# Sketched attention and a tanh-shrink layer pair: values loaded by head onto 96 partitions, q of the first batch split, and four small early reads

## The chip, the core and the metric

The kernel runs on one core of one Trainium2 chip. The core has a matrix engine (TensorE, PE in the profile), a vector engine (VectorE, DVE), a scalar engine (ScalarE, ACT), GpSimd (POOL), and SyncE (SP), which here only issues transfers; sixteen DMA engines move data between device memory and on-chip memory. The metric is the time of one execution in device microseconds, less is better.

## The reference

For four batches, four heads, 1088 tokens and head size 32, a linear attention with a sketched feature map comes first; its output, laid out as 4352 tokens of width 128, goes through two layers with h - tanh(h) between them.

```
def phi(x):                              # S1, S2: 8 x 32
    a = einsum('rd,bhsd->bhsr', S1, x)
    b = einsum('rd,bhsd->bhsr', S2, x)
    return einsum('bhsi,bhsj->bhsij', a, b).reshape(..., 64)
kv  = einsum('bhsf,bhsd->bhfd', phi(k), v)
z   = sum(phi(k), axis=2)
num = einsum('bhsf,bhfd->bhsd', phi(q), kv)
den = einsum('bhsf,bhf->bhs', phi(q), z)[..., None] + 1e-06
x   = (num / den).transpose(0, 2, 1, 3).reshape(4352, 128)
h   = x @ w_in                           # 128 x 2048
out = (h - tanh(h)) @ w_out              # 2048 x 128
```

All inputs and the output are float32.

## The kernel before

The kernel is a program of 753 operations, each put on one engine. The function `op` derives what each operation must wait for from the tiles that it reads and writes, `sync` turns that into semaphore waits, and `run` issues each engine's operations strictly in the order of a list (`ORDER`), which was written out beforehand by the planner in `schedule` from costs and due times. An engine that waits holds everything behind it in its list. Negative numbers in TensorE's list are idle matmuls on zeros.

**Loads.** All large loads are issued by SyncE in one queue: `load_k`, `load_q`, `load_v` for each batch, and four parts each of w_in and w_out (`load_w_in`, `load_w_out`). `load` keeps a list of the bytes asked for, `flow`, and makes a load wait until those more than 1,900,000 bytes ahead of it have landed (`AHEAD`). k and q come as 128 partitions (4 heads x 32 blocks j of 34 tokens), each one run of 4352 bytes; k of batch 0 comes in two parts. v comes in four transfers, one for each quarter c of the 34 tokens of a block: 32 partitions (the blocks j), and in each of them four heads with a run of nine tokens, 1152 bytes (seven tokens, 896 bytes, for the last quarter). On chip v lies as `vx`, partition 32 c + j, then head, token in the quarter, and 32 values. ScalarE's queue issues only the two small loads of S1 and S2 (`load_s`), ahead of the load of its tanh table.

**Attention.** k is transposed in 32 x 32 blocks by VectorE (L567, L710 for batch 0), projected by TensorE (L522), turned back (`kab`, L530), and multiplied out by GpSimd (`wk`, L558; for batch 0 partly VectorE); L585 sums `wk` against `vx`. q is transposed by VectorE (`q_transpose`, L608), projected (L624), turned back (`qf`, L631), and gives the denominators (`dt` L637, `den` L640, `rec` L643), the scaled factors (`an` L651), their products by GpSimd (`qp` L660), and the transposes of these (`qpT` L665). TensorE forms the numerators (L680), and ScalarE copies them to `xT` as bf16 (L690). The first 256 tokens of batch 0 have a short way of their own (`first_keys`, `first_factors`, `first_sums`, `first_numerators`; x at L799), so that the layers can start early; for them q of batch 0 is transposed in two parts (256 columns, then the rest), from one load. The copy to `sw` at L726 is a step of that way.

**Layers.** The tokens are cut into groups (128, 128, 256, seven of 512, 256). For each, 16 tiles of the first layer (L887) go to tanh on ScalarE (L892), 136 tiles of 128 x 512 in all, and the second layer (L906, L913 for the last group) sums w_out against tanh in one bank; the linear part h is taken care of by the product of the two weight matrices (`whi`, `wlo`; L932, L928). VectorE transposes each group's result out of the bank (L947, L940) and SyncE stores it (L954; the last group at L942). The next group's sums need that bank. w_in is cast by ScalarE (L819), w_out by GpSimd (L823).

Of the kernel before, what the change touches and what calls it, by code (L numbers as in the profile page):

```python
# [10 lines left out]
B, H, S, D = 4, 4, 1088, 32  # L11
# [5 lines left out]
OFF = (0, 9, 18, 27)  # L17
NT = 9
# [2 lines left out]

ORDER = {
    "tensor": (
# [17 lines left out]
    ),  # L41
    "scalar": (
# [9 lines left out]
    ),  # L52
    "vector": (
# [4 lines left out]
    ),  # L58
    "gpsimd": (
        21, 3, 22, 9, 7, 10, 8, 4, 23, 75, 82, 84, 59, 60, 134, 61, 62, 132, 150, 149, 151, 277, 302, 300, 280, 281,  # L60
        283, 285, 301, 431, 454, 456, 434, 435, 437, 439, 455, 579, 582, 583, 585, 587,
    ),
    "sync": (
# [4 lines left out]
    ),  # L68
}

# [256 lines left out]
def bass_polysketch_attn__then__act_tanh_shrink_kernel(nc, q, k, v, S1, S2, moe_w_in, moe_w_out, out):  # L327
    P = Program(nc)

    def sb(name, shape, dtype=F32):  # L330
        return nc.alloc_sbuf_tensor(name, shape, dtype).ap()
# [11 lines left out]
    identb = sb("identb", [128, 128], BF16)  # L343
    wz = sb("wz", [128, 512], BF16)
    spare = sb("spare", [128, 1], BF16)
    m4 = sb("m4", [128, 4])
    m16 = sb("m16", [128, 2, 4])
    e16 = sb("e16", [16, 8, 16])
# [7 lines left out]
    qraw = [sb(f"qraw{i}", [128, S]) for i in range(2)]  # L356
    kT = [sb(f"kT{i}", [128, 4 * NT * 32]) for i in range(2)]
    qT = [sb(f"qT{i}", [128, S]) for i in range(2)]
    vx = [sb(f"vx{i}", [128, H, NT, D]) for i in range(2)]
# [60 lines left out]
    def load_s():  # L420
        for i, src in enumerate((S2, S1)):
            load("scalar", ("s_raw",), "s", 0, lambda e, i=i, src=src: e.dma_start(
                out=s_raw[8 * i:8 * i + 8, :, :], in_=src[:, None, :].to_broadcast([R, H, D])), 4096, True, name="load s")

    def load_k(b, due):
        cuts = ((0, 512), (512, S)) if b == 0 else ((0, S),)
        for x, (lo, hi) in enumerate(cuts):
            load("sync", [("kraw", b % 2, y) for y in ((x,) if b == 0 else (0, 1))], f"k{b}{x}", due, lambda e, lo=lo, hi=hi: e.dma_start(  # L428
                out=kraw[b % 2][:, lo:hi], in_=k[b].rearrange("h (j c) d -> (h j) (c d)", j=32)[:, lo:hi]),
                512 * (hi - lo), rate=400 if b == 0 else 300, name=f"load k{b}")  # L430

    def load_v(b, due):
        src = v[b].rearrange("h (j c) d -> j h c d", j=32)
        for c in range(4):
            n = NT if c < 3 else 7
            load("sync", ("vx", b % 2), f"v{b}{c}", due + c, lambda e, c=c, n=n: e.dma_start(
                out=vx[b % 2][32 * c:32 * c + 32, :, 0:n, :].rearrange("j h t d -> j h (t d)"),
                in_=src[:, :, OFF[c]:OFF[c] + n, :].rearrange("j h t d -> j h (t d)")),
                128 * 128 * n, True, 226, name=f"load v{b}")

    def load_q(b, due):
        i = b % 2
        load("sync", ("qraw", i), f"q{b}", due, lambda e: e.dma_start(
            out=qraw[i][:, :], in_=q[b].rearrange("h (j c) d -> (h j) (c d)", j=32)), 512 * S, name=f"load q{b}")

    def load_w_in(x, due):
        load("sync", ("w_in_f", x), f"wi{x}", due, lambda e: e.dma_start(
            out=w_in_f[:, 512 * x:512 * x + 512], in_=moe_w_in[:, 512 * x:512 * x + 512]), 262144, rate=390, name="load w_in")
# [157 lines left out]
    def q_transpose(b, part, lo, hi):  # L606
        i = b % 2
        P.op("vector", dve(hi - lo), lambda e: e.transpose(out=qT[i][:, lo:hi], in_=qraw[i][:, lo:hi]),  # L608
             r=[("qraw", i)], w=[("qT", i, y) for y in (range(2) if part is None else (part,))], name="qT")

    def layout(nblk):
        nb = (nblk + 3) // 4
# [347 lines left out]
    constants()  # L960
    load_s()
    load_k(0, 100)
    load_q(0, 150)
    load_v(0, 200)
    load_w_in(0, 400)
    load_w_in(1, 450)
    load_w_in(2, 500)
    load_w_in(3, 550)
    load_w_out(0, 650)
    load_w_out(1, 700)  # L970
    load_k(1, 750)
# [14 lines left out]
    for kind, x in steps:  # L986
        x, upto = int(x), 0
# [22 lines left out]
        while g < len(groups) and sum(groups[g]) <= upto:  # L1010
            first_layer(g, *groups[g])
            if g < 2:
                turn_weights(g)
            elif g == 2:
                for y in range(3):
                    second_layer(y, *groups[y])
            else:
                second_layer(g, *groups[g])
            g += 1
    P.emit(lambda e: e.matmul(ps[:, 6, 0:128], wz[:, 0:128], wz[:, 0:128], start=True, stop=True))  # L1020


# [26 lines left out]
```

## Time and profile before

| what | value |
|---|---|
| time, median of 3 runs | 110.84 us (109.92 to 111.91) |
| time of the profiled execution | 111.44 us |
| its span | 109.7 us |
| granted TensorE clock | 0.998 |
| busy: PE, DVE, ACT, POOL | 101.0, 46.5, 84.4, 41.8 us |
| read from device memory, written | 8.79 MB, 2.23 MB |
| tanh on ScalarE (L892) | 136 tiles, 70.3 us |

Busy times are those of one execution; TensorE's are modelled, so a busy TensorE isn't one at its peak. In the stretches that follow, the columns are the stretch, its length, the busy time of PE, PEld (weight loads), DVE, ACT and POOL with the number of instructions, the granted clock, the share of time in which the sixteen DMA engines are busy, on average over them, and GB/s. In a timeline a row has the start, the busy time, the engine, the line, the operation, output and input, and in brackets the idle time ahead of it with what ended it. In the chain a row has the start, the duration and what it was. In the DMA issues the last number is the time from issue to landing.

### The profile page before, as it was taken

Reading aid. Unit: us, or ns where it says so; the run is one execution under the profiler, and the core shown is the slowest. Engines: PE = TensorE matmul, PEld = TensorE weight load, DVE = VectorE, ACT = ScalarE, POOL = GpSimd, SP = SyncE. Lnnn points to the kernel's source line nnn. Section 1 sums busy time; section 2 is a strip of 40 time slices with the busy share of each in tenths; the row PEclk is TensorE's granted clock in tenths of the full one; section 3 lists DMA queues with packets and bytes.
Section 4 is the critical chain, followed back from the end, with each engine's and each line's share of the span. In section 5 each row is a group of like instructions: output and inputs, shape, how many; then the busy total and the mean of one; then the engine's idle time right before and its main releaser. Section 6 shows DMA issues by size and latency. Waiting matters only on the chain.

```text
span 109.7 us, 3290 instructions
## 1 busy us (share of the span) xinstructions
PE 101.0 (92%) x1406; PEld 57.4 (52%) x1406; DVE 46.5 (42%) x88; ACT 84.4 (77%) x184; POOL 41.8 (38%) x46
## 2 busy tenths in 40 slices
PE   5999998898988989999999999999999999999940
PEld 4956677574646734443546543454444444345730
DVE  2737999736859384075017402527600200200210
ACT  3132479765964769798998979999979999999920
POOL 5204435799117998004999500269300000000000
PEclk9999999999999999999999999999999999999999
DMA  2999999996766821023000500410023041032061
GB/s 68 311 234 233 298 324 284 210 318 127 235 219 195 216 47 21 6 37 59 6 0 6 92 7 0 75 26 0 0 46 49 7 75 21 0 57 42 6 96 48
DMA packets 22195, 11.24 MB, mean 102 GB/s; under 512 B 17828, under 2 KB 20004, under 8 KB 22180
## 3 DMA queue, kind: packets, MB, share of 16 engines
q1 hardware_dynamic: 22100, 11.02, 40.9%
q8 instruction: 11, 0.18, 0.8%
q14 instruction: 4, 0.03, 0.1%
q10 hardware_dynamic: 80, 0.01, 0.1%
HBM read 8.79 MB, written 2.23 MB: 100 GB/s over the span
## 4 chain that ended last, share of the span: by engine, by line
PE 46%; DMA 32%; ACT 14%; DVE 2%; SPq 1%; issue 1%; DVEq 0%
PE ps L887 17%; PE ps L906 16%; DMA qraw<-in_q_dram 16%; ACT tt L892 13%; DMA w_out_f<-in_moe_w_out_dram 7%; DMA kraw<-in_k_dram 6%; PE ps L680 4%; DMA w_in_f<-in_moe_w_in_dram 4%; PE ps L932 2%; PE ps L585 2%; PE ps L913 1%; PE ps L624 1%; DVE qT L608 1%; ACT xT L690 1%; SPq L428 1%; PE ps L538 1%
## 5 line engine op out<-in xcount | busy, mean ns | idle before, releaser
L892 ACT ACTIVATE tt<-ps 128x512 bf16<-128x512 f32 x136 | 70.3, 659 | 4.8 <-PE ps L887 4.4
L887 PE MATMUL ps<-xT,w_in 128*128 128x512 bf16 (+2 forms) x176 | 48.1, 335 | 1.3 <-ACT w_inT L849 0.5
L906 PE MATMUL ps<-tt,w_out 128*128 128x512 bf16 (+2 forms) x160 | 41.3, 337 | 0.0
L887 PEld LDWEIGHTS ps<-xT,w_in 128*128 128x128 bf16 x176 | 17.5, 114 | 21.5 <-ACT tt L892 10.6
L947 DVE STREAM_TRANSPOSE osb<-ps 128x512 f32<-128x512 f32 (+2 forms) x10 | 5.9, 587 | 32.5 <-PE ps L906 32.5
L906 PEld LDWEIGHTS ps<-tt,w_out 128*128 128x128 bf16 x160 | 14.6, 99 | 9.1 <-ACT tt L892 0.7
L558 POOL TENSOR_TENSOR wk<-kab 128x768 f32<-128x768 f32 x10 | 15.1, 1508 | 8.9 <-DVE kab L530 8.3
L660 POOL TENSOR_TENSOR qp<-an,qf 128x768 f32<-128x768 f32 (+1 forms) x11 | 16.2, 1470 | 2.1 <-DVE an L651 1.3
L665 DVE STREAM_TRANSPOSE qpT<-qp 128x768 f32<-128x768 f32 (+1 forms) x12 | 11.1, 927 | 10.8 <-POOL qp L660 10.7
L637 POOL TENSOR_TENSOR dt<-qf 128x288 f32<-128x288 f32 x3 | 2.4, 796 | 16.8 <-DVE qf L631 16.8
L1020 PE MATMUL ps<-wz 128*128 128x128 bf16 x81 | 8.2, 256 | 0.0
L1020 PEld LDWEIGHTS ps<-wz 128*128 128x128 bf16 x81 | 6.4, 117 | 2.9 <-issue 2.6
L690 ACT CAST xT<-ps 128x256 bf16<-128x256 f32 (+3 forms) x16 | 5.3, 391 | 2.9 <-PE ps L680 2.9
L608 DVE STREAM_TRANSPOSE qT<-qraw 128x1088 f32<-128x1088 f32 (+2 forms) x5 | 5.4, 1072 | 3.0 <-DMA qraw<-in_q_dram 3.0
L680 PE MATMUL ps<-qpT,ndw 32*32 32x288 f32 (+1 forms) x256 | 6.2, 399 | 0.0
L631 DVE STREAM_TRANSPOSE qf<-ps 128x1152 f32<-128x1152 f32 (+1 forms) x4 | 5.2, 1307 | 0.8 <-PE ps L624 0.8
L567 DVE STREAM_TRANSPOSE kT<-kraw 128x1088 f32<-128x1088 f32 x3 | 3.9, 1297 | 2.1 <-DMA kraw<-in_k_dram 2.1
L680 PEld LDWEIGHTS ps<-qpT,ndw 32*32 32x32 f32 x256 | 3.2, 103 | 2.1 <-DVE qpT L665 0.6
L585 PEld LDWEIGHTS ps<-wk,vx 128*32 128x32 f32 x216 | 3.2, 110 | 1.9 <-issue 1.1
L530 DVE STREAM_TRANSPOSE kab<-ps 128x576 f32<-128x576 f32 (+2 forms) x5 | 3.1, 645 | 2.4 <-PE ps L522 2.4
L585 PE MATMUL ps<-wk,vx 128*32 128x64 f32 x216 | 4.1, 221 | 0.0
L538 PE MATMUL ps<-kab 128*64 128x32 f32 x72 | 3.1, 225 | 0.9 <-DVE kab L530 0.9
(97 smaller groups left out, 78.0 us busy)
## 6 DMA issues: line engine op xcount, KB each, us to landing
qraw<-in_q_dram SPq DMA_DIRECT2D x4, 544.0 KB, 5.9
vx<-in_v_dram SPq DMA_DIRECT2D x12, 144.0 KB, 6.7
kraw<-in_k_dram SPq DMA_DIRECT2D x3, 544.0 KB, 6.0
w_in_f<-in_moe_w_in_dram SPq DMA_DIRECT2D x4, 256.0 KB, 6.0
w_out_f<-in_moe_w_out_dram SPq DMA_DIRECT2D x4, 256.0 KB, 6.3
out_dram<-osb SPq DMA_DIRECT2D x16, 64.0 KB, 2.0
vx<-in_v_dram SPq DMA_DIRECT2D x4, 112.0 KB, 6.0
kraw<-in_k_dram SPq DMA_DIRECT2D x1, 288.0 KB, 3.2
```

Source lines behind the costliest of these rows:

```text
L558: P.op(eng, dve(64 * n) if eng == "vector" else pool(64 * n), lambda e: e.tensor_tensor(out=wk[i][:, t0:t1, :, :, :].rearrange("p t h i j ...
L585: ins = e.matmul(su[32 * h:32 * h + 32, 0:64], vx[b % 2][:, h, t, :], wk[i][:, t, h, :, :], start=(t == 0), stop=(t == NT - 1), tile_posit ...
L608: P.op("vector", dve(hi - lo), lambda e: e.transpose(out=qT[i][:, lo:hi], in_=qraw[i][:, lo:hi]), r=[("qraw", i)], w=[("qT", i, y) for y i ...
L660: e.tensor_tensor(out=qp[u][:, 4 * lo:4 * hi, :, :], in0=(pa if head else an[u][:, 4 * lo:4 * hi, :])[:, :, :, None].to_broadcast([128, m, ...
L665: P.op("vector", dve(64 * m), lambda e, lo=lo, hi=hi: e.transpose(out=qpT[u][:, :, 32 * lo:32 * hi].rearrange("p x (n j) -> p x n j", j=32 ...
L680: ins = e.matmul(ps[32 * h:32 * h + 32, c, 0:N], ndw[i][32 * c:32 * c + 32, y, 32 * h:32 * h + 32], qpT[u][32 * c:32 * c + 32, 2 * h + y, ...
L690: P.op("scalar", act(cols), lambda e: e.copy(dst, src), r=bank[c[0]:c[1]], w=[("x", (lo + 32 * first) // 32 + t) for t in range(cols // 32 ...
L887: ins = e.matmul(bk[:, n * y:n * y + n], w_tile(jb), xT[:, t0:t0 + n], start=True, stop=True)
L892: P.op("scalar", act(512), lambda e, ts=ts, bk=bk: e.activation(out=tt[:, ts, :], in_=bk, func=AF.Tanh, scale=-1.0), r=[kb], w=[("t", ts)] ...
L906: ins = e.matmul(acc[:, 0:n], w_out[:, jb, :], tt[:, ts, n * y:n * y + n], start=o.start and y == 0, stop=o.stop and y == per - 1)
L947: P.op("vector", dve(n), lambda e: e.transpose(out=osb[u][:, 0:n], in_=acc[:, 0:n]), r=[ka], w=[("osb", u, 0), ("osb", u, 1)], due=when(t0 ...
L1020: P.emit(lambda e: e.matmul(ps[:, 6, 0:128], wz[:, 0:128], wz[:, 0:128], start=True, stop=True))
```

## The change

There are four edits and a new order of issue.

- `load_v` loads by head: for each head one transfer of 96 partitions (three quarters c x 32 blocks j), each a run of nine tokens, 1152 bytes; then one transfer of 32 partitions for the last quarter of all heads, seven tokens each. That makes five transfers a batch instead of four. The layout of `vx` on chip doesn't change.
- q of batch 0 is loaded in two parts: the first 256 columns right after k, and the rest after w_in.
- `load_first` reads, on ScalarE's queue, sixteen rows of 64 bytes from each of q, v, w_in and w_out into a small tile that nothing reads. They stand after the loads of S1 and S2 and ahead of the tanh table.
- The planner's rates are changed (370 and 300 for v, 380 for q, 400 for k), and `ORDER` was made anew from them.

```diff
+    near = sb("near", [16, 4, 16])
...
+    def load_first(x):
+
+        src = (q[0].rearrange("h (j c) d -> (h j) (c d)", j=32), v[0].rearrange("h (j c) d -> (h j) (c d)", j=32),
+               moe_w_in, moe_w_out.rearrange("(p z) c -> p (z c)", p=128))[x]
+        load("scalar", ("near", x), f"out_n{x}", 1 + x, lambda e: e.dma_start(
+            out=near[:, x, :], in_=src.rearrange("(p y) c -> p y c", y=8)[:, 0, 0:16]), 1024, name="load t")
...
     def load_v(b, due):
-        src = v[b].rearrange("h (j c) d -> j h c d", j=32)
-        for c in range(4):
-            n = NT if c < 3 else 7
-            load("sync", ("vx", b % 2), f"v{b}{c}", due + c, lambda e, c=c, n=n: e.dma_start(
-                out=vx[b % 2][32 * c:32 * c + 32, :, 0:n, :].rearrange("j h t d -> j h (t d)"),
-                in_=src[:, :, OFF[c]:OFF[c] + n, :].rearrange("j h t d -> j h (t d)")),
-                128 * 128 * n, True, 226, name=f"load v{b}")
+        src = v[b].rearrange("h (j x) d -> h j x d", j=32)
+        for h in range(H):
+            load("sync", ("vx", b % 2), f"v{b}{h}", due + h, lambda e, h=h: e.dma_start(
+                out=vx[b % 2][0:96, h, :, :].rearrange("p t d -> p (t d)"),
+                in_=src[h, :, 0:27, :].rearrange("j (c t) d -> c j (t d)", c=3)),
+                96 * 1152, True, 370, name=f"load v{b}")
+        load("sync", ("vx", b % 2), f"v{b}4", due + 4, lambda e: e.dma_start(
+            out=vx[b % 2][96:128, :, 0:7, :].rearrange("j h t d -> j h (t d)"),
+            in_=src[:, :, 27:34, :].rearrange("h j t d -> j h (t d)")),
+            128 * 896, True, 300, name=f"load v{b}")
...
-    load_q(0, 150)
+    load_q(0, 150, 0)
     load_v(0, 200)
...
     load_w_in(3, 550)
+    load_q(0, 600, 1)
     load_w_out(0, 650)
...
+    for x in range(4):
+        load_first(x)
```

In the new lists the places that matter are these. SyncE: k0 in two parts, the first part of q0, v0 in five, w_in in four, the rest of q0, w_out 0 and 1, k1, w_out 2 and 3, v1 in five, q1, k2, v2 in five, q2, k3, q3, three groups' stores, v3 in five. Before, one group's stores stood ahead of q3. VectorE: the transpose of the rest of q0 stands after `dden` and ahead of `drec`; `wlo` stands behind the transpose of q1; then come the transposes of k2, of the first output group and of q2, `qf` of batch 1, the transposes of k3, of the second output group and of q3, `kab` of batch 2, and `den` and `rec` of batch 1. Before, `qf` of batch 1 stood ahead of the transposes of k3, of q2 and of q3, and `den` and `rec` of batch 1 ahead of that of q3. ScalarE: the cast of the first part of w_in stands ahead of the copy to `sw`. GpSimd: the four casts of w_out stand ahead of batch 0's `qp`, and one `wk` of batch 2, not two, ahead of batch 1's `an`.

More of the change, by code (lines that the diff above doesn't have):

```diff
@@ L23 @@
     "tensor": (
[17 rows of a table removed]
[17 rows of a table added]
     ),
     "scalar": (
[9 rows of a table removed]
[9 rows of a table added]
     ),
     "vector": (
[4 rows of a table removed]
[4 rows of a table added]
     ),
     "gpsimd": (
-        21, 3, 22, 9, 7, 10, 8, 4, 23, 75, 82, 84, 59, 60, 134, 61, 62, 132, 150, 149, 151, 277, 302, 300, 280, 281,
-        283, 285, 301, 431, 454, 456, 434, 435, 437, 439, 455, 579, 582, 583, 585, 587,
+        3, 22, 7, 21, 8, 4, 9, 10, 23, 78, 87, 85, 62, 63, 64, 65, 137, 135, 154, 153, 152, 281, 304, 284, 285, 287,
+        289, 305, 306, 436, 461, 439, 444, 440, 460, 442, 459, 584, 587, 588, 590, 592,
     ),
     "sync": (
[4 rows of a table removed]
[4 rows of a table added]
     ),
@@ L429, in load_k, with load_q @@
                 out=kraw[b % 2][:, lo:hi], in_=k[b].rearrange("h (j c) d -> (h j) (c d)", j=32)[:, lo:hi]),
-                512 * (hi - lo), rate=400 if b == 0 else 300, name=f"load k{b}")
+                512 * (hi - lo), rate=400, name=f"load k{b}")
     def load_v(b, due):
-        src = v[b].rearrange("h (j c) d -> j h c d", j=32)
-        for c in range(4):
-            n = NT if c < 3 else 7
-            load("sync", ("vx", b % 2), f"v{b}{c}", due + c, lambda e, c=c, n=n: e.dma_start(
-                out=vx[b % 2][32 * c:32 * c + 32, :, 0:n, :].rearrange("j h t d -> j h (t d)"),
-                in_=src[:, :, OFF[c]:OFF[c] + n, :].rearrange("j h t d -> j h (t d)")),
-                128 * 128 * n, True, 226, name=f"load v{b}")
-    def load_q(b, due):
+        src = v[b].rearrange("h (j x) d -> h j x d", j=32)
[8 more added lines that the diff above has]
+            128 * 896, True, 300, name=f"load v{b}")
+    def load_q(b, due, part=None):
         i = b % 2
-        load("sync", ("qraw", i), f"q{b}", due, lambda e: e.dma_start(
-            out=qraw[i][:, :], in_=q[b].rearrange("h (j c) d -> (h j) (c d)", j=32)), 512 * S, name=f"load q{b}")
+        lo, hi = ((0, S), (0, 256), (256, S))[0 if part is None else part + 1]
+        load("sync", [("qraw", i, y) for y in (range(2) if part is None else (part,))], f"q{b}{part}", due, lambda e: e.dma_start(
+            out=qraw[i][:, lo:hi], in_=q[b].rearrange("h (j c) d -> (h j) (c d)", j=32)[:, lo:hi]), 512 * (hi - lo), rate=380,
+            name=f"load q{b}")
     def load_w_in(x, due):
@@ L608, in q_transpose @@
         P.op("vector", dve(hi - lo), lambda e: e.transpose(out=qT[i][:, lo:hi], in_=qraw[i][:, lo:hi]),
-             r=[("qraw", i)], w=[("qT", i, y) for y in (range(2) if part is None else (part,))], name="qT")
+             r=[("qraw", i, y) for y in (range(2) if part is None else (part,))], w=[("qT", i, y) for y in (range(2) if part is None else (part,))], name="qT")
     def layout(nblk):
```

68 rows, old and new, of the table ORDER are left out of this document.

## The prediction

> **What bounds the kernel now.** I read the page's parts first (busy time, the costliest groups), then the stretches, the chain that ended last, and the DMA rows.
>
> ```profile
> L892 ACT ACTIVATE tt<-ps 128x512 bf16<-128x512 f32 x136 | 70.3, 659 | 4.8 <-PE ps L887 4.4
> 17.00:27.00 10.00, 8.45 (x183) 6.26 (x180) 6.60 (x9) 7.25 (x17) 7.89 (x7) 1.00 0.97 233
> 27.00:40.00 13.00, 11.67 (x211) 7.64 (x210) 9.54 (x13) 9.79 (x20) 7.50 (x7) 1.00 0.64 189
> 40.00:50.00 10.00, 10.00 (x139) 4.50 (x144) 4.10 (x5) 8.17 (x18) 4.03 (x4) 1.00 0.20 33
> 50.00:60.00 10.00, 10.00 (x148) 5.13 (x133) 4.00 (x6) 9.04 (x21) 8.25 (x7) 1.00 0.07 11
> 90.00:100.00 10.00, 9.92 (x47) 4.25 (x46) 0.72 (x1) 10.00 (x22) 0.00 (x0) 1.00 0.21 35
> ```
>
> The first row is ScalarE's tanh: 136 tiles, 70.3 us, so 0.52 us each. In the stretches the columns are PE, PEld, DVE, ACT, POOL, then the clock, the DMA engines' busy share and GB/s. From 50 us on ScalarE is 90 to 100% busy: there the tanh stream sets the pace, and what is late at its head comes out at the end. Before that it isn't full (7.25 of 10, 9.79 of 13, 8.17 of 10), and until 27 us the DMA engines are (0.97). The head depends on loads, and the chain says which:
>
> ```profile
> 1.28 0.41 SPq L428
> 1.73 7.26 DMA qraw<-in_q_dram
> ...
> 27.39 5.28 DMA qraw<-in_q_dram
> 32.69 4.83 DMA qraw<-in_q_dram
> 37.52 0.02 issue
> 37.54 1.31 DVE qT L608
> 38.85 0.34 DVE osb L947
> ...
> 43.52 1.53 PE ps L680 x63
> ```
>
> The q of batches 2 and 3 land at 32.67 and 37.52. VectorE takes its instructions in order, so the transposes of those q (L608) hold what is queued behind them. The last row is the numerators of batch 1. They feed the tiles from token 1088 on: ScalarE's list has 31 tanhs ahead of the copies that they release, and 105 behind. So **43.52 us is the mark to follow**: a shift of it is a shift of the end, less what ScalarE can regain later.
>
> **The change, part by part.** *Values by head.* Per batch, four transfers of 32 partitions become four of 96 (110,592 bytes each) and a tail of 32 partitions (114,688). The bytes are the same. What differs is the shape: the source is read as c, j, row with c = 3 outermost, while the destination is 96 partitions. The trace has one transfer of that build, the last store (L942): 128 partitions on one side, an outermost dimension of 4 on the other.
>
> ```profile
> 105.79 0.69 SPq L942 DMA_DIRECT2D out_dram<-osb  x1
> DMA packets 101, 0.10 MB, mean 86 GB/s; under 512 B 0, under 2 KB 101, under 8 KB 101
> 107.60:108.40 0.80, 0.00 (x0) 0.00 (x0) 0.00 (x0) 0.00 (x0) 0.00 (x0) 1.00 0.27 95
> 14.40:15.20 0.80, 0.80 (x31) 0.73 (x32) 0.80 (x2) 0.80 (x4) 0.61 (x1) 1.00 1.10 390
> GB/s 0 0 0 0 67 133 316 371 392 287 294 305 268 227 189 123 328 283 215 280 210 193 247 260 211 302 241 143 241 287 389 369 307 298 195 331 414 367 341 295
> ```
>
> While that store runs alone (the second row is from 107.4 to 108.6 us: rows of 1 KB, nothing else), the DMA share is 0.27 and the rate 95 GB/s: about 4 of 16 engines, 24 GB/s each. When all run, 390 GB/s / 16 is 24 as well. So the number of engines seems to follow the outermost dimension, 4 there and **3 in the new value loads**. I take 3. The other end is 16, if only the destination's 96 partitions count; in the store the 4 was on the destination's side, so the trace alone doesn't exclude that. The nearest row is the store, since no load here has unequal outer sizes.
>
> [...]
>
> With 3, those engines carry 4 x 110,592 / 3 = 147.5 KB of v per batch, and 7.2 KB of the tail, where an even spread is 34.8 KB: 120 KB more, at 24 GB/s 5.0 us per batch. Every other load has a sixteenth on each engine and waits for its part behind v. What the busiest engines carry after k0, in the new issue order, in KB: q0 first part 8.2, v0 154.6, w_in 65.5, q0 rest 26.6, w_out 65.5, k1 34.8 (sum 355.2, 14.8 us), v1 154.6, q1 34.8 (544.6, 22.7 us), k2 34.8, v2 154.6, q2 34.8 (768.8, 32.0 us). The anchor is k0's second part:
>
> ```profile
> kraw<-in_k_dram SPq DMA_DIRECT2D x1, 288.0 KB, 3.2
> ```
>
> issued at 1.28, landed at 4.5. So k1 lands at 19.3, q1 at 27.2 and q2 at 36.5 instead of 32.67. Loads are capped at 1.9 MB ahead: q3 with v3, k3 and q2 is 2.23 MB, so q3 is issued when q2 has landed, as the chain shows now (32.67, 32.69). With its 4.83 us it lands at 41.3 instead of 37.52.
>
> *Who waits.* These are VectorE's and GpSimd's rows on the way to the mark:
>
> ```profile
> 31.32 1.31 DVE L567 STREAM_TRANSPOSE kT<-kraw 128x1088 f32<-128x1088 f32 x1 [1.53 <-DMA kraw<-in_k_dram]
> 32.55 0.74 DVE L530 STREAM_TRANSPOSE kab<-ps 128x576 f32<-128x576 f32 x1
> 33.22 0.45 DVE L640 TENSOR_REDUCE den<-dt 128x36 f32<-128x324 f32 x1
> 34.81 0.33 DVE L643 RECIPROCAL rec<-den 128x36 f32<-128x36 f32 x1
> 35.06 0.25 DVE L947 STREAM_TRANSPOSE osb<-ps 128x128 f32<-128x128 f32 x1
> 33.38 3.09 POOL L558 TENSOR_TENSOR wk<-kab 128x768 f32<-128x768 f32 x2 [2.70 <-DVE kab L530]
> 36.61 0.68 POOL L651 TENSOR_TENSOR an<-qf,rec 128x288 f32<-128x288 f32 x1
> 37.37 4.68 POOL L660 TENSOR_TENSOR qp<-an,qf 128x768 f32<-128x768 f32 x3
> 42.09 0.98 DVE L665 STREAM_TRANSPOSE qpT<-qp 128x768 f32<-128x768 f32 x1 [0.61 <-POOL qp L660]
> 28.44 1.34 DVE L631 STREAM_TRANSPOSE qf<-ps 128x1152 f32<-128x1152 f32 x1
> ```
>
> The new list of VectorE is: transpose of q2, qf of batch 1, kT of k3, output transpose 1, transpose of q3, kab of batch 2, den, rec. So batch 1's factors, which started at 28.44, now stand behind q2, and its den and rec behind q3. From q2 at 36.5: 1.31 + 1.34 + 1.31 + 0.25 gives 40.7, so q3 (41.3) is later and decides. From 41.3: transpose 1.31, kab 0.74 (43.35), den 0.45, rec 0.33 (44.1). GpSimd now does one wk (3.09 / 2 = 1.55) after kab: 44.9. Then an 0.68 (45.6), qp 4.68 (50.3), the last qpT 0.98 (51.3), and the 0.45 that now lies between its end (43.07) and the numerators: **51.7 instead of 43.52, 8.2 us late**. ScalarE's new list has one tanh more ahead of the mark (32), worth 0.5. TensorE too is held, by output transpose 1, from about 34 to 41, since the next group's sums need its bank; what is left of group 3 after that (14 tanhs, 7.3 us) ends by 49 and so hides under the mark. Sum: +7.7 us.
>
> *The start.* ScalarE's cast of the first w_in part now stands ahead of the small copy to sw, and VectorE's transpose of the rest of q0 ahead of the reciprocal.
>
> ```profile
> 10.55 0.17 ACT L726 COPY sw<-ps 128x8 f32<-128x8 f32 x1 [1.12 <-PE ps L547]
> 11.75 1.26 ACT L819 CAST w_in<-w_in_f 128x512 bf16<-128x512 f32 x2 [1.04 <-DMA w_in_f<-in_moe_w_in_dram]
> 15.63 0.28 DVE L799 TENSOR_TENSOR xT<-ps,rT 128x128 bf16<-128x128 f32 x1
> ```
>
> The rest of q0 lands at 4.5 + 254.9 / 24 = 15.1; transpose 1.0, reciprocal 0.17 and one rT 0.27 put the first x at 16.6, a microsecond after 15.63. This I count as nothing, since TensorE has its wait of some 6 us at 34 to 41 behind it; without that cover it costs 1.
>
> *The early reads* add four issues on ScalarE's queue ahead of its table load.
>
> ```profile
> 0.80 0.91 ACTq L422 DMA_DIRECT2D s_raw<-in_S_dram  x2
> 1.74 1.28 ACT L459 ACT_TABLE_LOAD   x1 [1.74 <-PEq L1034]
> 5.49 0.21 ACT L505 COPY sw<-ps 128x64 f32<-128x64 f32 x1 [2.25 <-DVE sbd L501]
> SPq L447 <- DMA qraw<-in_q_dram: 3.7, 1, 3.7
> ```
>
> At 0.46 us each the table load ends at 1.74 + 1.82 + 1.28 = 4.8 and its activation of 0.21 at 5.1, ahead of the first use at 5.49: nothing, or 1.8 if that use came at once. What they gain lies between nothing and most of the excess of q0's 7.26 us over k0's 3.2, about 4 us on one landing; q0's first part isn't what is late when v runs on 3 engines, so I take nothing. Five more load issues up to batch 3 (four tails, one split) cost SP 0.43 each, 2.2 us, and 0.69 instead of 0.43 if a few-engine issue is dear; SP now waits 3.7 us for a landing at L447, which hides the early ones, and the full queue of the three engines hides the rest.
>
> The sum by the profiled execution: 111.44 (span 109.7 and 1.7 around it) + 7.7 = 119.1. It lies 0.6 over the median of 110.84, so I forecast **118.5**.
>
> **The rivals.** *Even spread:* the value loads run on all 16 engines, and the change does what it says. Now 17 to 27 us moves 233 GB/s at share 0.97, against 390 possible, and v's 32 partitions at a time may be why. At 390 a batch's 557 KB take 1.4 instead of 2.4 us, 2 us by q1; the split q0 lifts SP's wait of 3.7, of which I count half. The mark comes 3 to 4 us earlier: 107.5 (106 to 109.5). It decides if the DMA share stays near 1 in the first 25 us. Against it stands the store's 0.27. *Slip regained:* the three engines are as slow as I say, but ScalarE's idle time after 40 us (8.17, 9.04, and so on to 10.00; over six stretches of 10 us about 4.6 us) closes, since all later data lies ready: 118.5 - 4.6 = 113.9, and 111.5 with the fastest slice of the load rows, 414 / 16 = 26 GB/s, which brings q3 2.4 us forward. Against it: TensorE shows no idle time there, and the lists keep much the same mix.
>
> **How the numbers follow.** Even spread 0.12; slip regained 0.12; the forecast's case 0.76, in it 116 at 26 GB/s. Upwards, the loads now run at 233 / 16 = 15 GB/s per engine with all sixteen busy; by that q2 lands at 56 and the time is about 138. The store's row is nearer, three engines having the fabric nearly to themselves; half-way, 20 GB/s, q2 lands at 42.9 and the time is 125, which I take for the upper end, with 0.05 above. The range is 111.5 to 125 and leaves out the even spread and that tail. A measurement of this kernel can tell about 2% from no change (113.1 and 108.6 here): slower 0.82 (the forecast's case and half of the regained one), within 2% 0.08, faster 0.10.
>
> **What would show it.** Right: long stretches with a DMA share of about 0.2 to 0.4 and some 70 to 150 GB/s before 37 us, the 108 KB value loads landing 8 us and more after issue, VectorE waiting several us for q at L608, and batch 1's numerators after 49 us. Wrong at the first step: a share near 1 and 300 GB/s up to 15 us, and the numerators before 43. Wrong in size: numerators late but ScalarE over 97% busy from 52 us on. An engine rate well under 24 GB/s, or a queue that stops for everybody when one engine's part is full, would make it later than I say.

## The result, and the profile after

| what | before | after |
|---|---|---|
| median | 111.29 us (109.92 to 111.91, 4 runs) | **124.37 us** (123.58 to 125.11, 4 runs) |
| ratio, 95% interval | | 1.1266 [1.1122, 1.1411] |
| profiled execution (span) | 111.44 (109.7) us | 124.53 (122.8) us |
| granted TensorE clock | 0.998 | 0.928 |
| first x of the layers | 15.63 us | 20.50 us |
| q of batch 2 landed | 32.67 us | 39.45 us |
| numerators of batch 1 (the mark) start | 43.52 us | 56.27 us |
| from the mark to the end of the span | 66.2 us | 66.5 us |

The forecast was 118.5. The ratio is taken over the faster executions alone (two of the four before, 111.74 and 111.91 us, lie more than 1.5% above the fastest). The direction and the mechanism held, the size did not: the loss of 13 us by the medians, 14 by the ratio, is 1.7 or 1.8 times the 7.7 forecast. Line numbers are now those of the new source: by-head loads L443, tail L447, transposes of q L621, `qf` L644, key projection L535, `kab` L543, `den` L653, `rec` L656, `qp` L673, `qpT` L678, numerators L693, first layer L900, second L919, tanh L905.

The page of the changed kernel comes first: rates in 40 slices, then DMA issues with KB and time to landing.

```profile
DMA  3479685871861710203430032013003204022051
GB/s 113 143 221 295 189 276 217 246 219 76 251 204 76 206 21 0 48 3 95 105 69 0 5 59 34 0 31 57 2 0 59 35 15 71 0 41 47 5 80 48
...
vx<-in_v_dram SPq DMA_DIRECT2D x16, 108.0 KB
...
qraw<-in_q_dram SPq DMA_DIRECT2D x3, 544.0 KB, 8.2
```

The by-head loads have no landing time, just as the last store had none before, and a q of 544 KB takes 8.2 us (5.9 before). The trace's semaphore events say why. Each by-head load brings four increments, one soon after issue and three late (the first: 3.49, then 6.79, 6.89 and 6.90 us); every other large load brings 16. The last store brings one and four (in the kernel before at 106.86 and at 109.08 to 109.15), where its DMA share was 0.27 of sixteen, about 4 engines. So three late increments are three engines, and the packets agree: of the 29.5 us in which packets of 1152 bytes were in flight, 20.0 had exactly three of them and none had more than five; in the kernel before, 9.4 of 16.8 us had more than five. The value loads run on **three engines**.

The stretches (columns as before: PE, PEld, DVE, ACT, POOL, clock, DMA share, GB/s) and the chain that ended last:

```profile
36.00:38.00 2.00, 0.00 (x0) 0.00 (x0) 0.00 (x0) 0.00 (x0) 0.00 (x0) 0.72 0.23 83
38.00:40.00 2.00, 0.00 (x0) 0.00 (x0) 0.52 (x1) 0.00 (x0) 0.00 (x0) 0.50 0.18 74
40.00:42.00 2.00, 0.00 (x0) 0.00 (x0) 2.00 (x3) 0.00 (x0) 0.00 (x0) 0.50 0.75 215
44.00:46.00 2.00, 2.00 (x10) 1.32 (x9) 1.97 (x4) 1.00 (x2) 0.62 (x1) 0.50 0.21 33
46.00:48.00 2.00, 2.00 (x13) 1.22 (x11) 0.09 (x1) 0.69 (x2) 1.78 (x3) 0.72 0.00 0
```

```profile
21.00 8.17 DMA qraw<-in_q_dram
29.20 1.31 DVE qT L621
30.79 8.67 DMA qraw<-in_q_dram
39.48 1.31 DVE qT L621
40.79 1.28 DVE qf L644
42.11 1.22 PE ps L535 x16
...
56.27 1.53 PE ps L693 x63
```

From 36 to 39.4 us nothing computes, on any engine: the core waits for q of batch 2, while 0.18 of the sixteen engines (2.9) move 74 GB/s. When it has landed, VectorE does what is queued behind it, and only then can TensorE go on, at half clock. VectorE's timeline on the way to the mark:

```profile
39.48 1.31 DVE L621 STREAM_TRANSPOSE qT<-qraw 128x1088 f32<-128x1088 f32 x1 [7.29 <-DMA qraw<-in_q_dram]
40.72 1.34 DVE L644 STREAM_TRANSPOSE qf<-ps 128x1152 f32<-128x1152 f32 x1
...
43.37 1.27 DVE L621 STREAM_TRANSPOSE qT<-qraw 128x1088 f32<-128x1088 f32 x1
44.56 0.74 DVE L543 STREAM_TRANSPOSE kab<-ps 128x576 f32<-128x576 f32 x1
45.23 0.45 DVE L653 TENSOR_REDUCE den<-dt 128x36 f32<-128x324 f32 x1
45.71 0.38 DVE L656 RECIPROCAL rec<-den 128x36 f32<-128x36 f32 x1
...
52.53 0.98 DVE L678 STREAM_TRANSPOSE qpT<-qp 128x768 f32<-128x768 f32 x1 [0.61 <-POOL qp L673]
54.58 0.42 DVE L614 COPY ndw<-ps 128x256 f32<-128x256 f32 x1 [1.07 <-PE ps L609]
```

This is the chain of the forecast, in its order: wait for q2, `qf` behind it, q3, `kab`, `den`, `rec`, then GpSimd's products. One thing is new: the last transpose ends at 53.51, but the numerators start 2.76 us later, since TensorE is late with what the copy to `ndw` at 54.58 waits for.

### The profile page after: what moved, and what is told of

It is laid out like the page before. It is cut to its first block, busy times and chain, and to the rows that moved or that the text cites. A ratio compares the mean times of both kernels' runs of the same rounds, so it can differ in the third digit from the quotient of the medians.

```text
span 122.8 us, 3262 instructions
## 1 busy us (share of the span) xinstructions
PE 102.8 (84%) x1380; PEld 59.3 (48%) x1393; DVE 47.7 (39%) x88; ACT 84.2 (69%) x184; POOL 41.8 (34%) x46
## 4 chain that ended last, share of the span: by engine, by line
PE 47%; DMA 25%; ACT 14%; SPq 5%; DVE 4%; issue 2%; DVEq 0%
DMA qraw<-in_q_dram 20%; PE ps L900 17%; PE ps L919 15%; ACT tt L905 13%; DMA vx<-in_v_dram 5%; PE ps L693 4%; SPq L443 3%; PE ps L598 3%; PE ps L945 2%; DVE qT L621 2%; PE ps L926 2%; PE ps L535 2%; PE ps L637 1%; DVE qf L644 1%; ACT xT L703 1%
## 5 line engine op out<-in xcount | busy, mean ns | idle before, releaser
L905 ACT ACTIVATE tt<-ps 128x512 bf16<-128x512 f32 x136 | 70.3, 658 | 16.8 <-PE ps L535 8.2
L900 PE MATMUL ps<-xT,w_in 128*128 128x512 bf16 (+2 forms) x168 | 45.0, 335 | 1.6 <-issue 1.2
L919 PE MATMUL ps<-tt,w_out 128*128 128x512 bf16 (+2 forms) x155 | 40.9, 344 | 0.2 <-issue 0.2
L900 PEld LDWEIGHTS ps<-xT,w_in 128*128 128x128 bf16 x176 | 17.2, 115 | 19.3 <-ACT tt L905 10.7
L919 PEld LDWEIGHTS ps<-tt,w_out 128*128 128x128 bf16 x160 | 15.1, 102 | 10.8 <-issue 1.2
L673 POOL TENSOR_TENSOR qp<-an,qf 128x768 f32<-128x768 f32 (+1 forms) x11 | 16.2, 1471 | 4.1 <-DVE an L664 3.4
L678 DVE STREAM_TRANSPOSE qpT<-qp 128x768 f32<-128x768 f32 (+1 forms) x12 | 10.9, 919 | 10.2 <-POOL qp L673 10.2
L535 PE MATMUL ps<-kT,sbd 64*32 64x288 f32 x64 | 3.5, 505 | 7.5 <-DVE qf L644 7.5
L621 DVE STREAM_TRANSPOSE qT<-qraw 128x1088 f32<-128x1088 f32 (+2 forms) x5 | 5.4, 1071 | 8.0 <-DMA qraw<-in_q_dram 8.0
L644 DVE STREAM_TRANSPOSE qf<-ps 128x1152 f32<-128x1152 f32 (+1 forms) x4 | 5.2, 1306 | 5.5 <-PE ps L637 5.5
L693 PE MATMUL ps<-qpT,ndw 32*32 32x288 f32 (+1 forms) x256 | 6.2, 399 | 0.0
L832 ACT CAST w_in<-w_in_f 128x512 bf16<-128x512 f32 x4 | 2.5, 614 | 5.0 <-DMA w_in_f<-in_moe_w_in_dram 5.0
L752 PE MATMUL ps<-wk,vx 128*32 128x64 f32 x72 | 2.4, 314 | 4.0 <-DMA vx<-in_v_dram 4.0
L836 POOL CAST w_out<-w_out_f 128x512 bf16<-128x512 f32 x4 | 2.5, 613 | 8.8 <-DMA w_out_f<-in_moe_w_out_dram 8.7
L535 PEld LDWEIGHTS ps<-kT,sbd 64*32 64x32 f32 x64 | 0.8, 121 | 8.5 <-DVE qf L644 7.8
L598 PE MATMUL ps<-wk,vx 128*32 128x64 f32 x216 | 4.2, 221 | 0.0
```

The lines of the kernel that those rows point to most:

```text
L535: ins = e.matmul(ps[32 * c:32 * c + 32, r, 32 * t0:32 * t1], sbd[64 * r:64 * r + 64, 2 * r:2 * r + 2, :], kT[i][64 * r:64 * r + 64, 288 * ...
L598: ins = e.matmul(su[32 * h:32 * h + 32, 0:64], vx[b % 2][:, h, t, :], wk[i][:, t, h, :, :], start=(t == 0), stop=(t == NT - 1), tile_posit ...
L644: P.op("vector", dve(4 * N), lambda e: e.transpose(out=qf[u][:, 0:nb, :, :].rearrange("p n h x -> p h n x"), in_=ps[:, 0:4, 0:N].rearrange ...
L673: e.tensor_tensor(out=qp[u][:, 4 * lo:4 * hi, :, :], in0=(pa if head else an[u][:, 4 * lo:4 * hi, :])[:, :, :, None].to_broadcast([128, m, ...
L678: P.op("vector", dve(64 * m), lambda e, lo=lo, hi=hi: e.transpose(out=qpT[u][:, :, 32 * lo:32 * hi].rearrange("p x (n j) -> p x n j", j=32 ...
L693: ins = e.matmul(ps[32 * h:32 * h + 32, c, 0:N], ndw[i][32 * c:32 * c + 32, y, 32 * h:32 * h + 32], qpT[u][32 * c:32 * c + 32, 2 * h + y, ...
```

## The experiments

**1. The order of the source alone.** The changed kernel with one line changed. The destination stays at 96 partitions, but they are filled block by block, so a token's v lands beside another token's key features and the attention output differs.

```diff
-                in_=src[h, :, 0:27, :].rearrange("j (c t) d -> c j (t d)", c=3)),
+                in_=src[h, :, 0:27, :].rearrange("j (c t) d -> j c (t d)", c=3)),
```

> The changed kernel with one thing different: each value load reads its source as j, c, row instead of c, j, row, so that 32 is the outermost dimension instead of 3. The same bytes go to the same 96 partitions in the same runs, but the rows of the three quarters are interleaved over the partitions, so that the output is not the reference's. Three-engine theory: the loads run on 16 engines, the semaphore of each gets 16 landings instead of 3, q2 lands before 33 us, the numerators of batch 1 come at 39 to 43 us, and the time is 106 to 111 us. Rival (the new order and the early reads are what costs): it stays at 121 to 125 us. Rival (96 partitions of short runs are slow by themselves): 115 us and more with 16 landings.

111.59 us, ratio 1.0023 [0.994, 1.0106]. From its DMA issues, VectorE's timeline and the chain:

```profile
vx<-in_v_dram SPq DMA_DIRECT2D x16, 108.0 KB, 3.4
```

```profile
28.77 1.31 DVE L621 STREAM_TRANSPOSE qT<-qraw 128x1088 f32<-128x1088 f32 x1 [2.27 <-DMA qraw<-in_q_dram]
```

```profile
43.49 1.53 PE ps L693 x63
```

Sixteen increments a load, v of batch 0 all there at 7.30 us (13.54 in the changed kernel), and the 13 us are gone. So **the outermost dimension of 3 is the whole loss, and with the loads on sixteen engines the rest of the change is worth nothing**. The time lies 0.6 us over the range that I expected, and the mark 0.5. With q2 at 28.77, 3.9 us ahead of before, the mark is still at 43.49, as before (43.52). From the transpose of q2 to the mark it takes 14.72 us, without a wait for TensorE at `ndw`: the longer list behind q2 eats the gain here. The even-spread rival's 107.5 was wrong for that reason, which experiment 7 follows up.

**2. Values by quarter again.** The changed kernel with v on 32 partitions at a time, the last quarter in two transfers, so that five issues remain.

```diff
-        for h in range(H):
-            load("sync", ("vx", b % 2), f"v{b}{h}", due + h, lambda e, h=h: e.dma_start(
...
+        for x, (c, h0, h1) in enumerate(((0, 0, 4), (1, 0, 4), (2, 0, 4), (3, 0, 2), (3, 2, 4))):
+            n = NT if c < 3 else 7
...
```

> The changed kernel with the values by quarter as before (32 partitions a transfer; the last quarter in two, so that there are five transfers as the order wants). New order, split q and early reads stay. Three-engine theory: about the kernel before, 107 to 113 us, batch 1's numerators by 44 us. Rival (order or early reads cost): 118 us and more. Against the run with the source order changed it shows what 96 partitions are worth on 16 engines: nothing, or up to 2 us.

111.71 us, ratio 1.0021 [0.9928, 1.0114]; v of batch 0 landed by 8.04, 0.7 us after experiment 1. Batch 1's numerators came at 45.33, later than the 44 that I expected, but in an execution that took 113.90 us, the longest of the four. So 32 or 96 partitions make no difference to the time here (111.71 and 111.59 us), with sixteen engines carrying them in both.

**3. By-head values alone.** The kernel before with the new `load_v` and nothing else: old order of issue, old lists.

```diff
-        for c in range(4):
...
+        for h in range(H):
+            load("sync", ("vx", b % 2), f"v{b}{h}", due + h, lambda e, h=h: e.dma_start(
...
```

> The kernel before with the value loads by head alone (five transfers a batch in the place of four, nothing else changed: old order, q of batch 0 in one load, no early reads). Three-engine theory: q2 lands at 39 to 41 us here too, but batch 1's factors stand ahead of q2 on VectorE, so that the numerators come at 48 to 52 us and the time is 115 to 120 us. Rival (the new order is what costs): 110 to 113 us. If the order adds nothing to the delay: 122 to 126 us.

121.78 us, ratio 1.0947 [1.0878, 1.1016], a bit above the expectation. q2 landed at 39.94, as expected, and the numerators came 1.2 us later than expected; the granted clock is at a half from 37.1 to 47.4 us here too (experiment 5 has what that does). Its timeline and chain:

```profile
38.58 1.31 DVE L571 STREAM_TRANSPOSE kT<-kraw 128x1088 f32<-128x1088 f32 x1 [5.92 <-DMA kraw<-in_k_dram]
```

```profile
53.19 1.53 PE ps L684 x63
```

By-head loads cost 10.4 us in the old order (121.78 against 111.38 in the same comparison), where k of batch 3 is waited for. The rest of the change on top makes the time 2.6 longer (124.37); the differences that the traces show on the way are batch 1's `qf`, which ran at 31.33 here and at 40.72, behind q2, there, and its `den`, at 40.48 here and at 45.23, behind q3, there.

**4. Without the early reads, and with them alone.** The changed kernel without `load_first`, and the kernel before with it.

```diff
-    for x in range(4):
-        load_first(x)
```

> The changed kernel without the four early reads. Three-engine theory: they neither cost nor gain, 123.5 to 125.2 us. Rival (they save the first loads a stall): 125.5 us or more. Rival (four more issues on ScalarE's queue cost): 123 us or less.

> The kernel before with the four early reads alone. If first touches are what made its load of q0 take 7.3 us, that load lands by 7 us, VectorE's first transpose of q starts 2 us earlier and the time falls by 0.5 to 1.5 us. If not, 110.5 to 112 us, as before.

123.72 us, ratio 1.1192 [1.1064, 1.132], against 124.37 with them; and 112.02 us, ratio 1.0056 [0.9976, 1.0137]. VectorE in the second, at the first part of q0:

```profile
8.89 0.45 DVE L616 STREAM_TRANSPOSE qT<-qraw 128x256 f32<-128x256 f32 x1 [1.68 <-DMA qraw<-in_q_dram]
```

q0 lands at 8.86, 7.12 us after its issue; in the kernel before, it took 7.26. The four reads as placed gain nothing, and their issues cost nothing that can be told, as forecast. Whether a read that is complete before the load would shorten it isn't shown: the small read of q was issued at 1.75, just behind q0's load (1.74), and landed at 4.64. That q0's 7.3 us are the price of a first touch is unlikely all the same, since in the trace of experiment 3, without early reads, q0 took 4.91 us.

**5. TensorE kept busy in its waits.** The 2.76 us between the last transpose and the numerators might be half clock, or a mere backlog of matmuls. Idle matmuls on zeros, into a bank that the next sums overwrite, are to keep the clock up: 60 ahead of the first sums over v, and 130 ahead of batch 2's key projection.

```diff
+            def fill(e):
+                for _ in range(130):
+                    ins = e.matmul(ps[:, x, 0:128], wz[:, 0:128], wz[:, 0:128], start=True, stop=True)
+                return ins
+
+            P.op("tensor", 7000, fill, r=[("wz",)], w=[bank[x]], name="fill")
```

> The changed kernel with idle matmuls on zeros put where TensorE waits: 60 ahead of the first sums against v, 130 (some 7 us) ahead of the key projection of batch 2, where it waited from 34.6 to 42.1 us. They add no result. In the changed kernel the granted clock is at a half from about 37 to 47 us and from 13 to 19 us. If that half clock is what puts batch 1's numerators at 56.3 us instead of the 53.9 that the last transpose would allow, the clock stays at 1.0 and the time falls by 2 to 3.5 us, to 121 to 122.5 us. If TensorE's lateness comes from its waits alone, the time stays within 0.8 us of 124.4.

124.76 us: inconclusive. One execution kept a clock of 1.0 and took 122.12 us, the other three had 0.966 and took 124.68 to 125.27. In the profiled one (125.27) the idles ran from 38.12 to 45.55, so the projection, which could have started at about 42.5, started at 45.48. But from it to the numerators (57.26) it took 11.8 us, not 14.2. A second version had 60, then 25 ahead of the linear part of the first group, and 80:

```diff
-                for _ in range(130):
+                for _ in range((25, 80)[g - 2]):
```

> The changed kernel with idle matmuls on zeros where TensorE waits, this time 60 ahead of the first sums against v, 25 ahead of the linear part of group 0 (where it waits for wlo) and 80 instead of 130 ahead of the key projection of batch 2, since 130 ran on for 3 us after that projection could start (45.5 instead of 42.4 us). If the half clock after the long wait is the part of the delay that I missed, the stretch from that projection to batch 1's numerators shrinks from 14.2 us to about 12, the numerators come at 54 to 55 us and the time is 121.5 to 123 us. If it is TensorE's backlog alone, the stretch stays at 14 and the time at 124 to 125.

The median was 124.12 us, against the expectation. These idles ended at 39.94, 2.1 us before the projection, and the executions of this kernel differ in granted clock: the profiled one had 0.995 and took 122.17 us, the other three 0.973 to 0.984 and 124.1 to 126.2. In the profiled one the stretch from the projection (42.08) to the numerators (54.16) was 12.1 us, which is what I expected of the clock. The third version has 108 in place of 80:

> The changed kernel with idle matmuls on zeros in TensorE's waits, like the one before, but with 108 instead of 80 ahead of batch 2's key projection (their output goes to a bank that the next group's sums overwrite). At 0.058 us each from about 35.3 us they end near 41.6, just short of the 42.1 at which the projection could start, so that TensorE idles for less than 1 us instead of 2.1 and no useful work waits for them. If the half clock after the long wait is the term that the forecast missed behind the last transpose of the products: granted clock 0.99 or more in every execution, 12 us from the key projection to batch 1's numerators (14.2 without idles), these at 54 to 54.5, time 121.5 to 122.8. If the backlog of matmuls alone is the cause, and the clock isn't: numerators at 56, time 124 to 124.8.

**122.91 us** (122.53 to 123.21, 6 runs), ratio 1.1119 [1.1066, 1.1171]: all six lie under the fastest of the changed kernel's runs (123.58), at clocks of 0.986 to 1.0 (I had expected 0.99 or more) where those have 0.924 to 0.939. The median is 0.1 over what I expected. Eleven microseconds around the long wait, first in the changed kernel and then in this one:

```profile
36.00:47.00 11.00, 4.55 (x30) 2.44 (x32) 6.57 (x8) 1.08 (x2) 2.29 (x2) 0.54 0.32 92
```

```profile
37.00:48.00 11.00, 10.96 (x166) 9.10 (x166) 7.03 (x9) 3.36 (x7) 2.32 (x3) 1.00 0.31 90
```

Here are VectorE's transpose of q2, TensorE's projection and the numerators (the chain) in the third version:

```profile
40.42 1.31 DVE L622 STREAM_TRANSPOSE qT<-qraw 128x1088 f32<-128x1088 f32 x1 [7.30 <-DMA qraw<-in_q_dram]
```

```profile
43.16 0.72 PE L536 MATMUL ps<-kT,sbd 64*32 64x288 f32 x16
```

```profile
55.14 1.53 PE ps L694 x63
```

q2 came 0.94 us later in this execution than in the changed kernel's, so the mark must be counted from it: 14.72 us at full clock, 16.79 (39.48 to 56.27) at half. Experiment 1, never at half clock there, has 14.72 too (28.77 to 43.49), and the profiled execution of the second version 14.71 (39.45 to 54.16), so that a backlog alone doesn't explain the difference. The half clock is worth 2.07 us at the mark and 1.5 us in the medians (124.37 - 122.91).

**6. What the clock does.** No kernel of its own; the rows of the changed kernel's trace are TensorE's last work before the wait and its first after, and half microseconds around the two turns:

```profile
34.20 0.38 PE L900 MATMUL ps<-xT,w_in 128*128 128x256 bf16 x2
42.11 1.22 PE L535 MATMUL ps<-kT,sbd 64*32 64x288 f32 x16 [7.53 <-DVE qf L644]
```

```profile
36.50:37.00 0.50, 0.00 (x0) 0.00 (x0) 0.00 (x0) 0.00 (x0) 0.00 (x0) 0.90 0.25 78
37.00:37.50 0.50, 0.00 (x0) 0.00 (x0) 0.00 (x0) 0.00 (x0) 0.00 (x0) 0.50 0.21 73
...
46.50:47.00 0.50, 0.50 (x3) 0.24 (x2) 0.00 (x0) 0.00 (x0) 0.39 (x1) 0.50 0.00 0
47.00:47.50 0.50, 0.50 (x3) 0.23 (x2) 0.00 (x0) 0.18 (x1) 0.47 (x1) 0.86 0.00 0
```

The last matmul ended at 34.58 and the clock fell to half at 36.9, 2.3 us later; work came back at 42.11 and the clock at 47.1, 5.0 us later. The same sixteen projections took 1.22 us at half clock and 0.72 at full. The trace's record of the clock holds two values, 1.0 and 0.5, and has its changes at 13.00, 19.83, 36.90 and 47.14 us, apart by 6.83, 17.07 and 10.24, which is two, five and three times 3.41. Counted in such steps, TensorE was busy by its modelled records for 1.25 of the 3.41 us from 40.3 to 43.7, and for all of the next step, at whose end the clock came back. In the step from 33.5 to 36.9 it was busy for 1.08 us, and at its end the clock fell all the same. What decides when the clock turns isn't shown.

**7. Loads by quarter, order mended.** Where does a gain of 4 us at q2 go? Either to the new order, which has `qf` behind q2, or to the engines' own work. This is experiment 2 with the order mended: the rest of q0 behind the first x, batch 1's `qf` ahead of q2, its `den` and `rec` ahead of k3 and q3, its `an` and `qp` ahead of batch 2's `wk`. VectorE's list and GpSimd's, by operation numbers (TensorE's and ScalarE's follow with single moves):

```diff
-        92, 105, 93, 94, 95, 102, 127, 104, 128,
+        92, 93, 94, 95, 102, 104, 105, 127, 128,
...
-        313, 280, 452, 204, 462, 299, 282, 283, 219,
+        280, 313, 204, 282, 283, 452, 462, 299, 219,
...
-        281, 304, 284, 285, 287, 289, 305,
+        281, 284, 285, 287, 289, 304, 305,
```

> The kernel with values by quarter in the changed order, with the places mended that tied work to loads: on VectorE the transpose of the rest of q0 comes after the first x, batch 1's qf ahead of the transpose of q2, its den and rec ahead of those of k3 and q3; on GpSimd batch 1's an and qp come ahead of batch 2's first wk; TensorE's and ScalarE's lists follow (first projection of the rest and the spread a few places later). If the order ate what the earlier loads gained, the first x comes at 13 to 14.5 us instead of 15.6, batch 1's numerators at 40 to 42.5, and the time is 108 to 110 us, better than both kernels. Rival (ScalarE's and TensorE's own work sets the mark): 110.5 to 112.5 us.

112.55 us, ratio 1.0149 [0.998, 1.0317]. VectorE's last step ahead of the mark, and the chain:

```profile
42.88 0.42 DVE L612 COPY ndw<-ps 128x256 f32<-128x256 f32 x1 [2.59 <-PE ps L607]
```

```profile
44.57 1.53 PE ps L691 x63
```

The first x came at 14.78 instead of 13 to 14.5, and the mark at 44.57 instead of 40 to 42.5, so the time missed the expectation too. The last products are transposed at 40.3, 2.5 us earlier than in experiment 1, but the copy to `ndw` waits 2.59 us for TensorE. So mending the order frees VectorE's way, and then what stands ahead on TensorE's list holds the mark. No version ran faster than the kernel before.

## Where the prediction failed in its size, and where it was right

Two steps of the sum failed. The 24 GB/s per engine were too much for the value loads: they ran at 20.0, and q of batch 2 landed at 39.45 instead of 36.5 us. And TensorE's wait was put at nothing, since it hides under the mark; it brought half clock, which cost 2.07 us at the mark. The mechanism, three engines and VectorE held up behind a late q, is the one that the runs show.

- **Three engines, not sixteen: right.** Read from the store's share of 0.27, which did not exclude sixteen, so that the choice was my estimate; shown by the four increments of each load and by experiment 1, where the order of the source alone takes the whole loss away. That a batch's four loads share the same three engines, on which the 147.5 KB rests, the trace of the kernel before doesn't show; the changed kernel's increments do. The tail of v0 brought thirteen of its sixteen by 7.95 us and three from 13.28 to 13.55, the first part of w_in thirteen by 9.61 and three from 13.68 to 13.92, q2 thirteen by 34.71 and three from 38.90 to 39.46. Of the signs that I named, the low DMA share was only in part right: until 27 us the slices show 0.3 to 0.9, since the other thirteen engines moved their parts of the later loads meanwhile.
- **The rate of 24 GB/s an engine: too high, the first mis-sized term.** By landings (trace times), with the forecast's KB per busy engine:

| what the three engines carry | KB | from, to (us) | GB/s per engine |
|---|---|---|---|
| v0 with tail | 154.6 | 4.76, 13.54 | 17.6 |
| w_in, rest of q0 | 92.1 | 13.54, 16.89 | 27.5 |
| w_out, k1 | 100.3 | 16.89, 20.96 | 24.6 |
| v1 with tail | 154.6 | 20.96, 27.88 | 22.3 |
| q1, k2 | 69.6 | 27.88, 30.65 | 25.1 |
| v2 with tail | 154.6 | 30.65, 38.15 | 20.6 |
| q2 | 34.8 | 38.15, 39.45 | 26.8 |

  The value loads with their tails ran at 20.0 (463.8 KB in 23.2 us), all others at 25.8. At 24 those 463.8 KB would have taken 19.3, 3.9 us less; the others were 0.9 us faster than at 24. So q2 landed at 39.45 instead of 36.5. The forecast's upper end was a rate of 20 for everything; that the time came so near it is luck, since q2 came 3.5 us earlier than the 42.9 of that case, and the half clock made up for most of it.

  The premise of this term that did not hold is "three engines having the fabric nearly to themselves". By the trace's packets, from 20.97 to 24.0 us and from 30.65 to 32.0 (by their starts), a value packet of 1152 bytes took 51 ns, and the three engines moved 24.2 to 24.5 GB/s each, as in the store; from 24 to 26 and from 32 to 36.1 it took 62 to 69 ns, at 18.0 to 20.1 GB/s. The packets are the same size, so their size isn't the difference. In the slow stretches all other packets together kept 8.8 to 13.2 of the sixteen engines busy, in the fast ones 4.1 to 10.0. So the slow stretches are in the main those with more of the other packets; no run tests whether these are the cause.
- **Who waits: right, but for which load decides.** q2, `qf`, k3, q3, `kab`, `den`, `rec` and `qp` ran in that order. I had q3's landing (41.3) decide; it landed at 42.98, 3.5 us after its issue and not 4.83, while VectorE came to it at 43.37, so that q2 decided. From q2 to the mark the forecast had 15.2 us; at full clock it is 14.72, 0.48 less.
- **"The 14 tanhs end by 49, and 0.45 after the last transpose": the second mis-sized term.** I priced TensorE's wait from 34 to 41 as a delay that hides, at full speed. It ran 34.6 to 42.1, let the clock drop to half until 47.1, and left TensorE late at `ndw`: 2.76 us after the last transpose where experiment 5 has 0.69 (54.45 to 55.14). That is the 2.07 us.
- **A shift of the mark is a shift of the end: right.** 66.2 us before, 66.5 after, 66.3 in the third version of experiment 5 (121.4 - 55.14 = 66.26). So the rival *slip regained* fell: nothing was regained, nor did the one tanh more ahead of the mark give back its 0.5.
- **The sum.** At the mark 2.95 - 0.48 + 2.07 = 4.5 (measured 56.27 - 51.7 = 4.57); behind it 0.35, and the tanh's 0.5; and I had set the median 0.6 under the profiled execution, where it is 0.16 under: 0.44. Together 5.9, which is 124.37 - 118.5.
- **The start: right that it costs nothing, wrong by how much it slips.** The first x came at 20.50, not 16.6. I followed the rest of q0 only. TensorE's sums over v waited until 13.74 for the last of v0, the cast of w_in until 13.94 with the copy to `sw` behind it, and the granted clock was at a half until 19.8:

```profile
13.94 0.62 ACT L832 CAST w_in<-w_in_f 128x512 bf16<-128x512 f32 x1 [5.00 <-DMA w_in_f<-in_moe_w_in_dram]
20.50 0.29 DVE L812 TENSOR_TENSOR xT<-ps,rT 128x128 bf16<-128x128 f32 x1 [0.88 <-PE ps L806]
```

  The wait for q2 lies behind it and covers all of it: nothing computes from 36 to 39.4 us. That 4.9 us were covered, where I had counted on one, is luck.
- **The early reads, free: right** (experiment 4). **Even spread:** its price was wrong as well as its premise, since earlier loads don't bring the mark forward: in the new order it stays 14.72 us behind q2 (experiment 1), and with the order mended TensorE holds it (experiment 7).

## What to carry to other kernels

Look at the outermost dimension on both sides of a transfer: here the engine count went with it, 4 in the last store's destination (four late increments, a share of 0.27 of sixteen), 3 in the by-head loads' source (three late increments), and with 32 there, in experiment 1, sixteen increments. Writing the three quarters outermost in the source put 80% of v on three engines, and everything issued later queued behind them, for 13 us of 111. To size such a queue, don't take an engine's rate from a stretch in which few engines work: here 24 GB/s of a store that ran alone became 20.0 for loads beside others. And when a wait opens a hole on TensorE, like the 7.5 us here, price the half clock behind it too, 2 us at the mark.

## What was not expected of the hardware

Issuing a by-head load mostly took 0.70 to 0.74 us instead of 0.43. Part of that is the 96 partitions: in experiment 1, on sixteen engines, the median is 0.60. Single issues of batch 2 took up to 3.08 us, where experiment 1 has none over 0.94. So it comes with the three engines; what such an issue waits for, no run shows. These are SP's rows for batch 0 and batch 2, four issues each, and the tail of batch 2:

```profile
2.21 3.26 SPq L443 DMA_DIRECT2D vx<-in_v_dram  x4
22.64 6.13 SPq L443 DMA_DIRECT2D vx<-in_v_dram  x4
28.81 1.87 SPq L447 DMA_DIRECT2D vx<-in_v_dram  x1
```

SP issues everything, so such an issue holds up loads for the other thirteen engines too: q2 was issued at 30.79, 3.4 us later than before (27.39), though v2 on the three engines, until 38.15, decided when it landed. The value loads with their tails ran at 17.6 to 22.3 GB/s per engine, the loads in rows of 2 to 4 KB at 24.6 to 27.5. Since packets of one size ran at 18 and at 24.5, the row size alone can't be the reason; what slows them stays open.
